# Nyström attention and top-1 experts on one core: attention instructions in a written-out order, and q and k turned by the matrix engine

## The chip, the core and the metric

The kernel runs on one core of a Trainium2 chip. A core has five engines that run their own instruction streams in order and meet at semaphores: PE (TensorE, matrix products; its weight loads are listed apart as PEld), DVE (VectorE), ACT (ScalarE), POOL (GpSimd) and SP (SyncE, which only issues transfers here). PE's products go to PSUM, a small memory of its own that DVE and ACT read; the other data lie in SBUF. Transfers run on 16 DMA engines, issued from SP's queue and from POOL's.

The metric is the device time of one execution in microseconds (us). Before the change three runs gave 570.1, 567.15 and 567.03; the median is 567.15.

## The reference

```python
# q, k, v: (8 batches, 8 heads, 576, 64) f32;  m = 32 landmarks of g = 18 rows each
q_lm = q.reshape(B, H, m, S // m, D).mean(axis=3)
k_lm = k.reshape(B, H, m, S // m, D).mean(axis=3)
A  = softmax(scale * q    @ k_lm.T)      # 576 x 32
Bm = softmax(scale * q_lm @ k_lm.T)      # 32 x 32
C  = softmax(scale * q_lm @ k.T)         # 32 x 576
Z = Bm.T / (norm1(Bm) * norminf(Bm) + 1e-6)
for _ in range(6):
    Z = 2 * Z - Z @ Bm @ Z
x = (A @ Z @ C @ v)                      # then (8 * 576 tokens, 512)
...
e_idx = argmax(x @ w_gate, axis=1)       # 8 experts, each token goes to one
h = relu(x[mask] @ w1[e]); ye = h @ w2[e]
out[mask] = gate_w[mask, None] * sigmoid(x @ w_output_gate)[mask, e, None] * ye
```

## The kernel before

**Two stages.** The attention stage makes the rows of x and writes them to a DRAM table, `x_rows`; for each batch it also finds the tokens' experts. After the last batch a short routing part (L400 to L449) sorts the tokens by expert into 43 tiles of 128 slots. The expert stage gathers one tile after another from `x_rows` (L464, POOL's queue), multiplies it by `w1` and `w2` of the tile's expert (L483, L502, bf16) and scatters the result (L509).

**The unit of the attention stage** is a half-batch: four heads of one batch, so that 4 x 32 landmarks fill 128 partitions. There are 16 units. For each unit q and k are loaded as (head and landmark) x (18 x 64) into three shared slots `nats` (L178), and `turned` makes three things of each:

- `tr`, the 32x32 blocks turned by DVE (L180). It puts 32 of the 64 columns d on the partitions of a head, in two pieces c;
- the sums over the 18 rows of a landmark, five additions on POOL (L181 to L186), turned by DVE to `lmT` (L188);
- `bd`, the same four landmark blocks spread over a 128x128 block-diagonal matrix, two products with a mask on POOL (L191).

`scores` (L205) then multiplies `bd` (128x128) with `tr` (128x288) for two halves n and two pieces c. It is called for C (landmarks of q against k) and for A (landmarks of k against q). An f32 product stands in the trace as two MATMUL records, here called passes, each with its own weight load.

**The rest of a unit.** C: maximum on DVE (L247), exponential on ACT (L250), six turns on PE (L257) and copies on ACT (L258), then the product with v, 24 small products of 96x32 by 96x64 (L262). A: turn on DVE (L270), maximum (L272), subtraction on POOL (L276), exponential on ACT (L277), sum (L278), product on POOL (L280), turn back to `AT` (L282).

**Per batch**: `Bm` (L225 to L243), seven dependent Newton steps of two products (L295) and one DVE operation (L303) on both halves at once, `ZB` (L311, POOL), the gate's logits (L317 to L338), the choice of the expert and the token's place (L344 to L369), and five products `pX` with `ZB` (L393), each copied by ACT (L396) and sent to `x_rows` (L397, SP).

**Memory used twice.** `wall` holds the weights of all eight experts. Its last parts are free until they are loaded: q, k and the sums lie in expert 7's part, v in expert 6's. `load_expert` (L73 to L82, POOL's queue, two transfers of 1 MB written and 2 MB read) is called for experts 0 to 5 after batches 0 to 5, and for 6 and 7 after the last batch's `AT`. The expert stage picks its weights by an address from a register, so its first product waits for all eight loads.

**What sets the order.** A scheduling layer orders the instructions of each engine by the program's order and its own estimate of when operands and buffers are free; nothing in the program fixes it. PSUM buffers: one for the scores of C, one for those of A, one for the turns of C (`et`), two small ones (`m`), one for `pX`.

Of the kernel before, what the change touches and what calls it, by code (L numbers as in the profile page):

```python
# [22 lines left out]
F32 = mybir.dt.float32  # L23
BF16 = mybir.dt.bfloat16
EXP = mybir.ActivationFunctionType.Exp
SIG = mybir.ActivationFunctionType.Sigmoid
RELU = mybir.ActivationFunctionType.Relu
# [9 lines left out]
def kernel(  # L37
# [98 lines left out]
    s_bm = scale / (g * g)  # L136
    s_a = scale / g
    s_c = scale / g
    KC = g // 2
    NC = KC * m  # L140
    VJ = 6
    VA = g // VJ

    with tc.tile_pool(name="attn_c", bufs=1) as cp, \
# [17 lines left out]
        for G in Gs:  # L162
# [4 lines left out]
        nats = [wall[:, E - 1, i * 2 * GD:(i + 1) * 2 * GD].bitcast(F32).rearrange("p (k d) -> p k d", d=D)  # L167
                for i in range(3)]
        t9 = wall[:, E - 1, 6 * GD:7 * GD].bitcast(F32).rearrange("p (k d) -> p k d", d=D)
        VD = HH * VJ * D  # L170
        vSs = [wall[:VA * m, E - 2, i * 2 * VD:(i + 1) * 2 * VD].bitcast(F32).rearrange(
            "p (h j d) -> p h j d", h=HH, j=VJ) for i in range(2)]
        turns = iter(range(4 * B))

        def turned(src, b, hf):

            nat = nats[next(turns) % 3]
            nc.sync.dma_start(out=nat, in_=src[b, hf * HH:(hf + 1) * HH].rearrange("h (r k) d -> (h r) k d", k=g))  # L178
            tr = sb.tile([128, g, 2, m], F32, tag="tr", bufs=3)
            nc.vector.transpose(out=tr.rearrange("p k c r -> p (k c r)"), in_=nat.rearrange("p k d -> p (k d)"))  # L180
            nc.gpsimd.tensor_tensor(t9, nat[:, 0:9], nat[:, 9:18], op=ADD)  # L181
            nc.gpsimd.tensor_tensor(t9[:, 0:4], t9[:, 0:4], t9[:, 4:8], op=ADD)
            nc.gpsimd.tensor_tensor(t9[:, 0:2], t9[:, 0:2], t9[:, 2:4], op=ADD)
            nc.gpsimd.tensor_tensor(t9[:, 0], t9[:, 0], t9[:, 1], op=ADD)
            lm = sb.tile([128, D], F32, tag="lm")
            nc.gpsimd.tensor_tensor(lm, t9[:, 0], t9[:, 8], op=ADD)  # L186
            lmT = sb.tile([128, 2, m], F32, tag="lmT", bufs=4)
            nc.vector.transpose(out=lmT.rearrange("p c r -> p (c r)"), in_=lm)  # L188
            bd = sb.tile([128, 2, HH, m], F32, tag="bd", bufs=4)
            for c in range(2):  # L190
                nc.gpsimd.tensor_tensor(  # L191
                    bd[:, c], mask,
                    lmT[:, c, :].rearrange("p (h r) -> p h r", h=1).to_broadcast([128, HH, m]), op=MUL)
            return tr, lmT, bd

        def scores(bd, tr, tag, by_j=False):

            p = ps.tile([128, 2, 512], F32, tag=tag)
            for n in range(2):
                for c in range(2):  # L200
                    if by_j:
                        rhs = tr.rearrange("p (a j) c r -> p j a c r", j=VJ)[:, n * VJ // 2:(n + 1) * VJ // 2, :, c, :]
                    else:
                        rhs = tr[:, n * KC:(n + 1) * KC, c, :]
                    nc.tensor.matmul(p[:, n, :NC], lhsT=bd[:, c].rearrange("p h r -> p (h r)"),  # L205
                                     rhs=rhs, start=(c == 0), stop=(c == 1))
            return p[:, :, :NC]

        for b in range(B):
            XW = sb.tile([128, 2, 128 + D], F32, tag="X", bufs=3)  # L210
            cc = sb.tile([128, 2], F32, tag="cc")
            ATs = []
            for hf in range(2):
                vS = vSs[hf]
                for a in range(VA):
                    nc.sync.dma_start(
                        out=vS[a * m:(a + 1) * m],
                        in_=v[b, hf * HH:(hf + 1) * HH].rearrange("h (r k) d -> r h k d", k=g)[:, :, a * VJ:(a + 1) * VJ, :])
                qT, qlmT, qBD = turned(q, b, hf)
                kT, klmT, kBD = turned(k, b, hf)  # L220


                pB = ps.tile([128, 192], F32, tag="m", bufs=2)
                for c in range(2):
                    nc.tensor.matmul(pB[:, :m], lhsT=qBD[:, c].rearrange("p h r -> p (h r)"),  # L225
                                     rhs=klmT[:, c, :], start=(c == 0), stop=(c == 1))
                st = sb.tile([128, 8], F32, tag="st", bufs=4)
                nc.vector.tensor_reduce(st[:, 0:1], pB[:, :m], axis=X, op=MAX)
                nc.vector.tensor_scalar(out=st[:, 1:2], in0=st[:, 0:1], scalar1=-s_bm, scalar2=None, op0=MUL)
                Bm = sb.tile([128, m], F32, tag="Bm")  # L230
                nc.scalar.activation(out=Bm, in_=pB[:, :m], func=EXP, scale=s_bm, bias=st[:, 1:2],
                                     accum_out=st[:, 2:3])
                nc.vector.reciprocal(st[:, 3:4], st[:, 2:3])
                nc.vector.tensor_scalar(out=Bm, in0=Bm, scalar1=st[:, 3:4], scalar2=None, op0=MUL)
                nc.gpsimd.tensor_tensor(
                    XW[:, hf, :128].rearrange("p (h r) -> p h r", r=m), mask,
                    Bm.rearrange("p (h r) -> p h r", h=1).to_broadcast([128, HH, m]), op=MUL)
                pS = ps.tile([128, 192], F32, tag="m", bufs=2)
                nc.tensor.matmul(pS[:, :m], lhsT=bones, rhs=Bm)
                nc.vector.tensor_reduce(cc[:, hf:hf + 1], pS[:, :m], axis=X, op=MAX)  # L240
                nc.vector.tensor_scalar(out=cc[:, hf:hf + 1], in0=cc[:, hf:hf + 1], scalar1=1e-6,
                                        scalar2=None, op0=ADD)
                nc.vector.reciprocal(cc[:, hf:hf + 1], cc[:, hf:hf + 1])  # L243


                pC = scores(qBD, kT, "sc", by_j=True)
                nc.vector.tensor_reduce(st[:, 4:5], pC, axis=mybir.AxisListType.XY, op=MAX)  # L247
                nc.vector.tensor_scalar(out=st[:, 5:6], in0=st[:, 4:5], scalar1=-s_c, scalar2=None, op0=MUL)
                EC = sb.tile([128, VJ, VA * m], F32, tag="EC", bufs=1)
                nc.scalar.activation(out=EC.rearrange("p (n j) q -> p n (j q)", n=2), in_=pC, func=EXP,  # L250
                                     scale=s_c, bias=st[:, 5:6], accum_out=st[:, 6:7])
                nc.vector.reciprocal(st[:, 7:8], st[:, 6:7])
                ECT = sb.tile([VA * m, VJ, 128], F32, tag="ECT", bufs=1)
                for j3 in range(2):
                    pE = ps.tile([VA * m, VJ // 2, 128], F32, tag="et")
                    for j in range(VJ // 2):
                        nc.tensor.transpose(pE[:, j, :], in_=EC[:, j3 * (VJ // 2) + j, :], identity=I128)  # L257
                    nc.scalar.copy(ECT[:, j3 * (VJ // 2):(j3 + 1) * (VJ // 2), :], pE)  # L258
                pV = ps.tile([128, 192], F32, tag="m", bufs=2)
                for j in range(VJ):  # L260
                    for h in range(HH):
                        nc.tensor.matmul(pV[h * m:(h + 1) * m, :D], lhsT=ECT[:, j, h * m:(h + 1) * m],  # L262
                                         rhs=vS[:, h, j, :], start=(j == 0), stop=(j == VJ - 1))
                nc.vector.tensor_scalar(out=XW[:, hf, 128:], in0=pV[:, :D], scalar1=st[:, 7:8],
                                        scalar2=None, op0=MUL)


                pA = scores(kBD, qT, "sa")
                At = sb.tile([128, g, m], F32, tag="At")
                nc.vector.transpose(out=At.rearrange("p (n k) r -> p n (k r)", n=2), in_=pA)  # L270
                ax = sb.tile([128, 2, g], F32, tag="ax")
                nc.vector.tensor_reduce(ax[:, 0], At, axis=X, op=MAX)  # L272

                def b_l(ap):
                    return ap.rearrange("p (k r) -> p k r", r=1).to_broadcast([128, g, m])
                nc.gpsimd.tensor_tensor(At, At, b_l(ax[:, 0]), op=SUB)  # L276
                nc.scalar.activation(out=At, in_=At, func=EXP, scale=s_a)  # L277
                nc.vector.tensor_reduce(ax[:, 1], At, axis=X, op=ADD)  # L278
# [5 lines left out]
            if b < E - 2:  # L284
                load_expert(b, ATs[1])
            elif b == B - 1:
                load_expert(E - 2, ATs[1])
                load_expert(E - 1, ATs[1])
# [264 lines left out]
```

## Time and profile before

| | us |
|---|---|
| median of three runs | 567.15 |
| the profiled execution | 568.91 |
| its span, first to last instruction | 567.2 |
| first q loaded, first work on it | 15.14 |
| first score product (L205) | 20.4 |
| `ZB` of batch 0 and of batch 7 (L311) | 64.2 and 347.0 |
| first gather of the expert stage (L464) | 368.6 |
| first product of the expert stage (L483) | 374.0 |

Busy time over the span: PE 438.5 us (77%), DVE 285.8 (50%), ACT 122.0 (22%), POOL 305.1 (54%). The granted clock of TensorE is 0.872 on average.

A line of the windows view gives a stretch, its length, then each engine's busy time with the number of instructions, the granted clock, the share of the DMA engines and GB/s. A line of the timeline gives start, duration, engine, source line, operation, output<-input, shape, and how many records were merged (x4); in brackets stands the idle time before it and what ended it. A line of the groups gives the busy time and the mean ns of one, then the idle time before and its releasers.

### The profile page before, as it was taken

The numbers are of one execution on the slowest core, as the hardware profiler recorded it, in microseconds if no ns is written. First come the engines' busy times: TensorE is split into PE (matmuls) and PEld (weight loads), VectorE is DVE, ScalarE is ACT, GpSimd is POOL, SyncE is SP. The second block draws the span as 40 slices with busy tenths as digits, with TensorE's granted clock in tenths as the row PEclk, the third lists the DMA queues.
The fourth block names the chain that finished last, engine by engine and source line by source line (L and its number), as shares of the span: only waits on it lengthen the run. The fifth ranks groups of instructions, "written<-read, shape, count | busy, mean of one in ns | idle before, by whom it ended". The sixth has DMA issues, their size and how long they took to land. (4 is left out here: it accounts for less than half of the span.)

```text
span 567.2 us, 9257 instructions
## 1 busy us (share of the span) xinstructions
PE 438.5 (77%) x3127; PEld 277.0 (49%) x3127; DVE 285.8 (50%) x748; ACT 122.0 (22%) x279; POOL 305.1 (54%) x492
## 2 busy tenths in 40 slices
PE   0458758758776867779797878559999999999992
PEld 0235545536555545448474554325555555555551
DVE  1355557657666756736764322713444444353441
ACT  0012222123131222122231211112223222232220
POOL 2667895796687678585624111353444545454422
PEclk9978969969897958877897565769999999999998
DMA  6643946935989369388044754121232323223200
GB/s 163 168 125 84 210 119 180 213 107 118 254 195 206 100 167 218 103 156 184 9 111 68 126 92 72 33 75 57 75 112 85 107 81 104 86 92 94 85 29 0
DMA packets 41726, 66.13 MB, mean 117 GB/s; under 512 B 10353, under 2 KB 29810, under 8 KB 41682
## 3 DMA queue, kind: packets, MB, share of 16 engines
q0 software_dynamic: 18048, 31.90, 26.3%
q1 hardware_dynamic: 23634, 33.64, 21.5%
q8 instruction: 27, 0.44, 0.4%
q14 instruction: 17, 0.14, 0.1%
HBM read 67.58 MB, written 16.56 MB: 148 GB/s over the span
## 5 line engine op out<-in xcount | busy, mean ns | idle before, releaser
L205 PE MATMUL p<-tr,bd 128*128 128x288 f32 x256 | 88.6, 474 | 28.5 <-DVE tr L180 21.1
L509 POOL DMA_INDIRECT out_dram<-ysb x43 | 43.5, 1012 | 93.7 <-DVE ysb L508 90.0
L483 PE MATMUL ph<-wall,xT 128*128 x344 | 82.9, 385 | 3.0 <-DVE xT L471 2.9
L502 PE MATMUL py<-wall,hT 128*128 x344 | 81.1, 379 | 0.0
L393 PE MATMUL pX<-ZB,AT 128*128 128x256 f32 (+1 forms) x160 | 63.4, 520 | 19.8 <-ACT xo L396 15.2
L487 ACT ACTIVATE h<-ph 128x512 bf16<-128x512 f32 x86 | 46.7, 594 | 144.7 <-PE ph L483 141.6
L205 PEld LDWEIGHTS p<-tr,bd 128*128 128x128 f32 x256 | 52.9, 222 | 41.4 <-POOL bd L191 29.7
L295 PE MATMUL pN<-nxt 128*128 128x192 f32 x192 | 47.8, 375 | 19.9 <-DVE nxt L303 16.8
L483 PEld LDWEIGHTS <-xT 128*128 128x128 bf16 x344 | 33.9, 99 | 45.3 <-issue 5.7
L393 PEld LDWEIGHTS pX<-ZB,AT 128*128 128x128 f32 (+1 forms) x160 | 32.7, 233 | 44.1 <-ACT xo L396 23.1
L181 POOL TENSOR_TENSOR wall<-wall 128x576 f32<-128x576 f32 x32 | 44.9, 1402 | 13.7 <-DMA wall<-in_q_dram 11.3
L295 PEld LDWEIGHTS pN<-nxt 128*128 128x128 f32 x192 | 34.8, 209 | 33.7 <-DVE nxt L303 26.6
L464 POOL DMA_INDIRECT xs<-x_rows,gat_i x43 | 41.9, 974 | 15.9 <-issue 13.4
L180 DVE STREAM_TRANSPOSE tr<-wall 128x1152 f32<-128x1152 f32 x32 | 43.3, 1352 | 12.4 <-DMA wall<-in_q_dram 11.5
L502 PEld LDWEIGHTS <-hT 128*128 128x128 bf16 x344 | 31.9, 98 | 30.7
L495 DVE COPY hT<-pht 128x1024 bf16<-128x1024 bf16 x43 | 29.7, 690 | 29.4 <-PE pht L493 23.2
L507 DVE CAST ysb<-xs 128x1 int32<-128x1 f32 x43 | 6.6, 154 | 74.7 <-issue 64.6
L191 POOL TENSOR_TENSOR bd<-mask,lmT 128x128 f32<-128x128 f32 x64 | 28.0, 456 | 25.2 <-PE p L205 11.8
L508 DVE TENSOR_SCALAR ysb<-py,xs 128x512 f32<-128x512 f32 x43 | 31.9, 743 | 4.2 <-PE py L502 3.8
L396 ACT CAST xo<-pX 128x512 bf16<-128x512 f32 (+1 forms) x40 | 23.3, 581 | 49.9 <-PE pX L393 34.4
L303 DVE SCALAR_TENSOR_TENSOR nxt<-nxt,pN 128x384 f32<-128x384 f32 x40 | 21.5, 538 | 17.9 <-PE pN L295 17.7
L276 POOL TENSOR_TENSOR At<-At,ax 128x576 f32<-128x576 f32 x16 | 18.4, 1157 | 21.1 <-DVE ax L272 21.1
(136 smaller groups left out, 607.3 us busy)
## 6 DMA issues: line engine op xcount, KB each, us to landing
wall<-in_moe_w_dram POOLq DMA_DIRECT2D x16, 1024.0 KB
wall<-in_v_dram SPq DMA_DIRECT2D x48, 192.0 KB, 4.2
wall<-in_q_dram SPq DMA_DIRECT2D x16, 576.0 KB, 5.1
wall<-in_k_dram SPq DMA_DIRECT2D x16, 576.0 KB, 5.2
x_rows<-xo SPq DMA_DIRECT2D x32, 128.0 KB, 2.8
xs<-x_rows,gat_i POOLq DMA_INDIRECT x43
out_dram<-ysb POOLq DMA_INDIRECT x43
x_rows<-St SPq DMA_DIRECT2D x1, 516.0 KB, 4.6
```

Of the source, the lines that this page charges most:

```text
L180: nc.vector.transpose(out=tr.rearrange("p k c r -> p (k c r)"), in_=nat.rearrange("p k d -> p (k d)"))
L181: nc.gpsimd.tensor_tensor(t9, nat[:, 0:9], nat[:, 9:18], op=ADD)
L205: nc.tensor.matmul(p[:, n, :NC], lhsT=bd[:, c].rearrange("p h r -> p (h r)"), rhs=rhs, start=(c == 0), stop=(c == 1))
L295: nc.tensor.matmul(pN[:, hf, :], lhsT=cur[:, hf, :128], rhs=cur[:, hf, :])
L393: nc.tensor.matmul(pX[:tk, hf * HH * D:(hf + 1) * HH * D], lhsT=ATs[hf][:, j * 128:j * 128 + tk], rhs=ZB[:, hf].rearrange("p h d -> p (h d)"))
L464: nc.gpsimd.indirect_dma_start(out=xs, out_offset=None, in_=x_rows, in_offset=bass.IndirectOffsetOnAxis(ap=gat_i[:, j:j + 1], axis=0))
L483: nc.tensor.matmul(ph[hf], lhsT=xT[:, dc, :], rhs=wf[:, bass.ds(we[j] + (dc * F + hf * 512), 512)], start=(dc == 0), stop=(dc == DCH - 1))
L487: nc.scalar.activation(out=hs[j][:, hf * 512:(hf + 1) * 512], in_=ph[hf], func=RELU)
L495: nc.vector.tensor_copy(hTs[j], pht)
L502: nc.tensor.matmul(py, lhsT=hT[:, fc, :], rhs=wf[:, bass.ds(we[j] + (W1 + fc * HD), HD)], start=(fc == 0), stop=(fc == FCH - 1))
L508: nc.vector.tensor_scalar(out=ysb[:, :HD], in0=py, scalar1=xs[:, HD // 2:HD // 2 + 1], scalar2=None, op0=MUL)
L509: nc.gpsimd.indirect_dma_start(out=out, out_offset=bass.IndirectOffsetOnAxis(ap=token, axis=0), in_=ysb[:, :HD], in_offset=None, bounds_ch ...
```

## The change

The arithmetic stays; where and when it is done changes.

- The instructions of the attention stage are cut into pieces (`turn3`, `c_scores`, `a_max`, `p_mm` and so on). Each piece gets a place on a time axis with a period P = 12.0 for a unit, and the pieces are issued in the order of their places under `manual_schedule()`, so that every engine's order is the program's. Unit u's q and k are turned during unit u-1's scores, the Newton steps of a batch run in the next two units, the logits and `pX` two units later.
- q and k are turned by PE: nine 128x128 turns each (`turn3`), three to a PSUM buffer, copied by ACT (`keep3`). A turned pair of rows has 64 columns d on 64 partitions, twice.
- The sums of k stay on POOL, those of q go to DVE (`sums`); both landmark sets are turned by PE (`turn_lm`) and scaled by ACT (`keep_lm`). `bd` and its products are gone.
- `scores` is eight products with 64 contracted rows and 32 output columns each, 288 long: two row halves by four heads, in 64x32 tiles of the array.
- Six slots for q and k instead of three (experts 7's and 5's parts); `AT` lies in expert 4's part. Experts 0 to 3 are loaded after units 1, 3, 5 and 7, experts 5, 6, 7 after the last unit, expert 4 after the last `pX`.
- PSUM buffers: two for turns (`t`), one for all scores (`s`), two small ones (`m`), one for the Newton steps (`n`), one for `pX`. Some small DVE operations are done for both halves at once; the scaling of v's product moves from DVE to ACT.

```diff
-        def turned(src, b, hf):
-            nat = nats[next(turns) % 3]
...
+        nats = [home(E - 1 - i // 3 * 2, i % 3, GD).rearrange("p (k d) -> p k d", d=D) for i in range(6)]
+        t9s = [home(e, 6, GD // 2).rearrange("p (k d) -> p k d", d=D) for e in (E - 1, E - 3)]
...
+        def sums(u, i):
+            eng, t9, nat = (nc.gpsimd, nc.vector)[i], t9s[i], nats[(2 * u + i) % 6]
+            eng.tensor_tensor(t9, nat[:, 0:9], nat[:, 9:18], op=ADD)
+            eng.tensor_tensor(t9[:, 0:4], t9[:, 0:4], t9[:, 4:8], op=ADD)
+            eng.tensor_tensor(t9[:, 0:2], t9[:, 0:2], t9[:, 2:4], op=ADD)
+            eng.tensor_tensor(t9[:, 0], t9[:, 0], t9[:, 1], op=ADD)
+            lm[u, i] = sb.tile([128, 2, D], F32, tag=f"lm{i}", name="lm")
+            eng.tensor_tensor(lm[u, i], t9[:, 0:1].to_broadcast([128, 2, D]), t9[:, 8:9].to_broadcast([128, 2, D]), op=ADD)
+        def turn3(u, i, n):
+            nat = nats[(2 * u + i) % 6]
+            if n == 0:
+                tr[u, i] = sb.tile([128, K2, 128], F32, tag="tr", bufs=4, name="tr")
+            tr[u, i, n] = pT = ps.tile([128, 3, 128], F32, tag="t", bufs=2, name="pT")
+            for k2 in range(3):
+                nc.tensor.transpose(pT[:, k2], identity=I128,
+                                    in_=nat[:, 6 * n + 2 * k2:6 * n + 2 * k2 + 2].rearrange("p k d -> p (k d)"))
+        def keep3(u, i, n):
+            nc.scalar.copy(tr[u, i][:, 3 * n:3 * n + 3], tr.pop((u, i, n)))
...
+        def scores(lms, tr, by_j=False):
+            p = ps.tile([128, 2, 512], F32, tag="s")
+            for h in range(HH):
+                for i in range(2):
+                    rhs = tr[i * D:(i + 1) * D, :, hm(h)]
+                    if by_j:
+                        rhs = rhs.rearrange("p (a c) r -> p c a r", a=VA)
+                    nc.tensor.matmul(p[hm(h), i, :NC], lhsT=lms[i * D:(i + 1) * D, hm(h)], rhs=rhs)
+            return p[:, :, :NC]
...
+        P = 12.0
+        for u in range(NU):
+            t = u * P
+            at(t - 4 * P + 11.9 if u > 2 else -30 + u, load_qk, u)
+            at(t - 2 * P + 11.9 if u > 1 else -30 + u + 0.5, load_v, u)
+            for n in range(3):
+                at(t - P + 1.5 + 0.4 * n, turn3, u, 0, n)
+                at(t - P + 2.6 + 0.5 * n, keep3, u, 0, n)
+                at(t - P + 4.9 + 0.4 * n, turn3, u, 1, n)
+                at(t - P + 5.5 + 0.5 * n, keep3, u, 1, n)
+            at(t - P + 0.1, sums, u, 0)
+            at(t - P + 1.9, sums, u, 1)
+            at(t - P + 8.5, turn_lm, u)
+            at(t - P + 8.9, keep_lm, u)
+            at(t + 0.0, c_scores, u)
+            at(t + 0.8, c_max, u)
+            at(t + 1.6, c_exp, u)
+            at(t + 3.5, a_scores, u)
+            at(t + 4.3, a_max, u)
+            at(t + 5.9, a_sub, u)
+            at(t + 7.1, a_exp, u)
+            at(t + 7.9, a_sum, u)
+            at(t + 9.0, a_mul, u)
+            at(t + P + 0.2, a_back, u)
+            for i in range(2):
+                at(t + 6.1 + 0.4 * i, c_turn, u, i)
+                at(t + 7.8 + 0.5 * i, c_keep, u, i)
+            at(t + 8.8, values, u)
+            at(t + 9.8, keep_values, u)
...
+        for b in range(B):
+            t = (2 * b + 1) * P
...
+            t += P
+            for it, place in enumerate((0.7, 4.2, 7.8, 10.5, 12.7, 16.2, 19.8)):
+                at(t + place, p_mm, b, it)
+                at(t + place + 0.9, p_next, b, it)
...
+            at(t + 2.8, logits, b)
+            at(t + 6.2, choose, b)
...
+            for j, place in enumerate((6.9, 9.8, P + 2.8, P + 6.9, P + 9.7)):
+                at(t + place, x_mm, b, j)
+                at(t + place + 1.0, x_out, b, j)
+        for e in range(E):
+            u = 2 * e + 1 if e < E - 4 else NU - 1
+            at((NU + 4) * P if e == E - 4 else u * P + P + 3.3, lambda e=e, u=u: load_expert(e, ATs[u]))
+        with tc.manual_schedule():
+            for _, _, fn, args in sorted(plan, key=lambda p: p[:2]):
+                fn(*args)
```

## The prediction

> **What bounds the kernel now.** The chain of waits ends in the last transfers and covers 0.7% of the span, so it says nothing of the attention stage. I read the windows first, cutting the span where the two stages meet.
>
> ```profile
> 15.00:374.00 359.00, 257.67 (x1927) 180.55 (x1928) 205.11 (x561) 74.03 (x192) 220.86 (x392) 0.81 0.60 136
> 374.00:567.00 193.00, 180.79 (x1200) 96.50 (x1199) 78.39 (x169) 46.67 (x86) 81.26 (x82) 0.98 0.24 78
> 333.00:346.00 13.00, 9.25 (x23) 6.71 (x24) 3.50 (x7) 0.00 (x0) 0.57 (x1) 0.50 0.99 161
> ```
>
> The columns are PE, PEld, DVE, ACT, POOL, clock, DMA share, GB/s. The expert stage (193 us) is bound by PE and the change doesn't touch it. In the attention stage no engine is full: POOL is busy 62%, PE 72% with unfinished pipelines counted, at a clock of 0.81. Next the pace, from the instructions of one line:
>
> ```profile
> L311 POOL TENSOR_TENSOR ZB<-mask,nxt x16: 712/726/731, 64.2 to 347.7; 128x256 f32<-128x256 f32 x16
> ```
>
> Batch 0's first ZB starts at 64.2, batch 7's at 347.0: 7 batches, 40.4 us each, **20.2 us per unit** (half-batch). Divided by 16 units the busy times are POOL 13.8, DVE 12.8, ACT 4.6. So waits between engines bound the stage: the fullest engine, POOL, works 68% of a period. PE's true load I take from starts in the timeline where it waits for nothing and the clock is full:
>
> ```profile
> 263.50 1.13 PE L205 MATMUL p<-tr,bd 128*128 128x288 f32 x4
> 264.48 0.49 PE L257 MATMUL pE<-I,EC 128*96 128x128 f32 x3
> 264.80 0.65 PE L205 MATMUL p<-tr,bd 128*128 128x288 f32 x2
> 265.29 0.81 PE L295 MATMUL pN<-nxt 128*128 128x192 f32 x4
> 265.94 0.49 PE L257 MATMUL pE<-I,EC 128*96 128x128 f32 x3
> ...
> 287.39 1.03 PE L393 MATMUL pX<-ZB,AT 128*128 128x256 f32 x4
> 288.26 0.65 PE L205 MATMUL p<-tr,bd 128*128 128x288 f32 x2
> ```
>
> From start to start: a score pass 0.98/4 = 0.245, a turn 0.32/3 = 0.107, a Newton pass 0.65/4 = 0.163, a pX pass 0.87/4 = 0.217. The tail of a group lies under the next one.
>
> **PE's load per unit, before and after.** Before: 16 score passes 3.9; 6 turns 0.64; 14 Newton passes 2.28; 10 pX passes 2.17; v's product 1.04 (two fences down); logits, gates, ranks and the like (half of L332's 1.28, of L324's 0.27 and of five small groups of 0.1 to 0.25) 1.15; pB 0.45. Sum 11.6. After, the score passes and pB's four go. Added are 18 turns of q and k, 2 of the landmarks, and two score calls. The trace shows no 128-column turn: 0.107 (the 96-column row) below, 0.107 x 128/96 = 0.143 above; I take 0.128, so 18 are 2.3 and 2 are 0.25. No 64x32 tile with 288 columns is there either; the nearest rows are small products side by side:
>
> ```profile
> 261.23 1.10 PE L262 MATMUL pV<-wall,ECT 96*32 96x64 f32 x48
> 262.27 0.59 PE L295 MATMUL pN<-XW 128*128 128x192 f32 x2
> ...
> 348.97 0.34 PE L324 MATMUL pG<-wgs,ZT 64*32 64x16 f32 x16
> 349.24 1.22 PE L393 MATMUL pX<-ZB,AT 128*128 128x256 f32 x2
> ```
>
> 48 passes of 64 columns take 1.04 us, 0.022 each, where one alone would need 0.245 x 64/288 = 0.054; and 16 of the 64x32 form are through in 0.27, at half clock. So tiles overlap. A call has 16 passes on 8 tiles: two rounds of 0.245 if all eight overlap, plus 0.2 for getting in and out (below the 0.27), 0.69; if none did, 3.9. I take 0.69, since the 64x32 row is the same form; two calls 1.4. After: 2.3 + 0.25 + 1.4 + 0.64 + 2.28 + 2.17 + 1.04 + 1.15 = **11.2**. PE's work hardly falls; the gain must come from waits.
>
> **The other engines per unit, after.** Rows used:
>
> ```profile
> L181 POOL TENSOR_TENSOR wall<-wall 128x576 f32<-128x576 f32 x32 | 44.9, 1402 | 13.7 <-DMA wall<-in_q_dram 11.3 <-DMA wall<-in_k_dram 0.8
> L180 DVE STREAM_TRANSPOSE tr<-wall 128x1152 f32<-128x1152 f32 x32 | 43.3, 1352 | 12.4 <-DMA wall<-in_q_dram 11.5 <-PE p L205 0.8
> L258 ACT COPY ECT<-pE 96x384 f32<-96x384 f32 x32 | 15.1, 473 | 31.1 <-PE pE L257 30.6 <-PE prk L357 0.4 <-PE pV L262 0.2
> ```
>
> *DVE* loses two turns (2 x 1.35) and two of lmT (0.48), gains q's sums: by the 0.74 of a 576-long operation (L272), 0.54 of 384 (L303) and 0.28 of 128 (L306), the five cost 0.74 + 0.40 + 0.27 + 0.20 + 0.27 = 1.9. With what stays (C's maximum 0.75, A's turns and reductions 3.3, Newton 1.75, routing and Bm 2.7) 10.5. *POOL* loses q's sums (1.40 + 0.73 + 0.46 + 0.33 + 0.32 = 3.2) and four bd products (1.8): 13.8 - 5.0 = 8.8. *ACT* gains six copies of 0.47, lmT's 0.4 and v's scaling 0.25: 8.1. *DMA*: q, k and v unchanged; six slots start them two units ahead.
>
> **The period.** In the written order all four engines fit in 12. I laid PE's order of an even unit on these prices and found where it must wait. Turns have two buffers, so the third group of k's turns waits for the first ACT copy, which stands behind C's exponential: 0.95. The third group of q's waits likewise: 0.4. C's turns wait for the same buffers: 0.2. v's product waits for the second ECT copy, which stands behind A's exponential and an xo copy: 0.45. Sum 2.0. Behind PE's wait stand pX and the Newton pass, so DVE is late with it.
>
> One wait is new: DVE's five q additions run beside POOL's five for k.
>
> ```profile
> 353.12 0.20 DVE L349 TENSOR_TENSOR oh<-row,sm 128x40 bf16<-128x40 f32 x1
> ...
> 284.04 0.82 DVE L349 TENSOR_TENSOR oh<-row,sm 128x40 bf16<-128x40 f32 x1
> ...
> 283.58 1.21 POOL L280 TENSOR_TENSOR At<-At,ax 128x576 f32<-128x576 f32 x1
> ```
>
> The same DVE instruction takes 0.20 with POOL idle and 0.82 beside a POOL operation that ends at 284.79. Bounds: 0 if they miss each other, half of POOL's 3.3 = 1.65 if each addition meets one. Behind them stands A's maximum, and POOL, ACT and PE behind that; the order leaves some slack there, I take 0.3. The Trainium skill, "SBUF — State Buffer", Who interferes with whom, says that a DVE tensor_tensor with both inputs in SBUF takes a port shared with GpSimd and the later one blocks fully; the row agrees, and by it alone I would book all 1.65, 21 us more over 16 units.
>
> *Clock.* In slices of 10 us the clock is 0.52 where PE is busy 5.5 (200 to 210) and 0.91 at 9.8 (260 to 270); in the expert stage 1.00. PE's true duty was 11.6/20.2 = 0.57 at a mean clock of 0.86 from 60 to 300; at 11.2/14.3 = 0.78, on the line to 1.00 at full duty, the clock is 0.93: 11.2/0.93 = 12.0. Bounds: 11.2 (clock 1) and 13.8 (0.81, the whole stage's). The Trainium skill, "TensorE: Matmul & The Clock Gate", Part 4: PE-mode transpose, speaks against the change: turns don't count as a busy array in the same way. By it the duty without turns is (11.2 - 3.2)/14.3 = 0.56, the clock stays 0.86, and a unit needs 13.0: 16 us more in the end. No run here shows f32 turns in such a share; bf16 turns are 12 of 28 PE instructions of the expert stage, at 1.00.
>
> Period 12.0 + 2.0 + 0.3 = **14.3**; bounds 12.0 (every wait hidden) and 13.8 + 2.0 + 1.65 = 17.4.
>
> **Before and after the periods.** k is now first on SP's queue, at 4.8 instead of v's pieces; with 5.2 to landing it is there at 10, q at 11.5; turns, copies and lmT take 4.5, so the first scores come at 16 (before 20.4). Units 0 and 1 have no Newton or pX yet: -6.
>
> At the end two paths race. *Compute*: seven Newton steps at
>
> ```profile
> 335.75 1.65 PE L295 MATMUL pN<-nxt 128*128 128x192 f32 x4 [0.65 <-DVE nxt L303]
> 338.11 1.65 PE L295 MATMUL pN<-nxt 128*128 128x192 f32 x4 [0.70 <-DVE nxt L303]
> ```
>
> 2.3 each at half clock = 16, +0.7 to begin, +5 for batch 6's pX in between; from the last step to the first gather 368.63 - 346.67 = 22, to PE 3.1: 47. *Weights*: four experts now wait for the last unit, where before there were two. The windows' third line is one expert's load alone: 13 us at a share of 0.99. The first expert product waits for all of them: 2.5 + 4 x 13 + 2 to land = **56.5** after the last period. This load was under the Newton steps before; now it is the bound, and compute has 9.5 of slack. Then 193.2 of expert stage (374.0 to the end).
>
> **Sum** against the profiled execution: 1.7 around the span + 16 - 6 + 16 x 14.3 + 56.5 + 193.2 = 490.2, where it has 568.91. The median is 1.8 lower: **488**.
>
> **Rivals.**
> - *The timetable holds at its 12 us.* For: DVE, POOL and ACT fit. Against: PE's 2 us of waits. 1.7 + 10 + 192 + 56.5 + 193.2 - 1.8 = 452. Chance 0.15.
> - *A fixed order waits as the scheduler's did.* PE at 68% of 12.0/0.68 = 17.6: 541. For: one late instruction stops its whole engine. Chance 0.12.
> - *The clock stays at half in the stage; slower.* PE then needs 22.4 + 2.0 = 24.4 a unit: 650. For: 320 to 350, clock 0.50 with PE busy 75%, waits of 0.7 between products. Against: PE would then be full, and full slices have 1.00. It decides from a period of 19.2, a mean clock of 0.66. Chance 0.08.
> - *The 64x32 tiles don't overlap.* 2 x 3.2 more a unit, 20.7: 590. Against: the L324 rows. Chance 0.04.
>
> The forecast, periods of 13 to 16.5, has 0.58; 0.03 is left for what I don't see. 0.5% is about what a measurement of this kernel tells from no change. Faster 0.86, the same 0.02, slower 0.12. Range: 452 (period 12.0) to 538 (period 17.4).
>
> **What would show it.** ZB 28 to 29 us apart per batch; score groups of 16 records within 0.7 to 0.9; DVE's q additions at 1.9 or stretched towards 3.5; PE idle before the third turn group, put down to ACT's copy; clock near 0.93; the first expert product released by a transfer into `wall`, with PE idle some 10 us. Wrong if PE's clock falls with the turns, or if periods differ from unit to unit by more than 3 us.

## The result, and the profile after

The changed kernel takes 469.9 us (468.1 to 473.1, 4 runs) where the kernel before took 568.6 in the same job: a ratio of 0.826, 95% interval 0.820 to 0.833. A second job gave 472.0 us and 0.829 (0.825 to 0.833); that second job is the yardstick for the variants below. The forecast was 488 us with a range of 452 to 538.

The profiled execution took 473.05 us. Its page begins with the busy time of each engine, its share of the span and the instructions; of the slices (a fortieth of the span each, busy share in tenths) these are PE's, DVE's, POOL's and the granted clock's:

```profile
span 471.3 us, 10353 instructions
...
PE 388.6 (82%) x3729; PEld 242.5 (51%) x3751; DVE 264.2 (56%) x676; ACT 166.2 (35%) x383; POOL 233.6 (50%) x348
...
PE   0878888888888898898685438999999999999991
...
DVE  1266787878879787987445403443444434444441
...
POOL 2566667483857547373811551444445545554231
PEclk9987999999999999999986559999999999999996
```

PE now has eights and nines from the fourth slice to the nineteenth, and from the fifth on the clock stands at nine beside them; before, no engine was full in that stage. The dip in slices 20 to 24 is the tail between the attention and the expert stage. The same in windows (PE, PEld, DVE, ACT, POOL, clock, DMA share, GB/s):

```profile
19.00:230.00 211.00, 179.02 (x2387) 125.33 (x2372) 161.48 (x415) 107.92 (x272) 127.90 (x207) 0.98 0.70 179
230.00:284.00 54.00, 29.15 (x161) 18.61 (x161) 20.30 (x72) 8.14 (x19) 21.74 (x41) 0.68 1.07 197
284.00:471.00 187.00, 174.70 (x1164) 94.67 (x1184) 77.86 (x166) 45.59 (x84) 77.72 (x78) 0.98 0.24 76
261.00:282.00 21.00, 6.75 (x51) 4.37 (x52) 4.47 (x13) 0.58 (x1) 12.11 (x13) 0.50 1.01 197
```

The stage of 16 units takes 211 us, where before they took some 323 (16 x 20.2). The last line lies in the tail: the transfers fill it at 197 GB/s while no engine is full (POOL, the busiest, works 12.1 of the 21 us). The pace, from one line's instructions (duration least/median/most in ns, first and last start):

```profile
L368 POOL TENSOR_TENSOR ZB<-mask,ZV x16: 723/730/736, 65.4 to 244.6; 128x256 f32<-128x256 f32 x16
```

Batch by batch ZB starts at 65.4, 92.7, 119.9, 147.2, 174.2, 201.3, 226.3 and 244.0: some 27.1 us apart until the work runs out, **13.56 us a unit** from unit 5 to unit 15 by C's exponentials (81.9 to 217.5). One odd unit on PE (start, us, instructions, idle before and what ended it):

```profile
190.17 0.87 PE L210 MATMUL pT<-I,wall 128*128 128x128 f32 x6
191.90 0.55 PE L210 MATMUL pT<-I,wall 128*128 128x128 f32 x3 [0.86 <-ACT tr L214]
192.28 1.03 PE L482 MATMUL pX<-ZB,wall 128*128 128x256 f32 x4
193.24 0.72 PE L234 MATMUL p<-tr,lmT 64*32 64x288 f32 x16
...
195.70 0.55 PE L210 MATMUL pT<-I,wall 128*128 128x128 f32 x3 [0.24 <-ACT tr L214]
...
199.41 0.41 PE L219 MATMUL pM<-I,lm 128*128 128x128 f32 x2 [0.55 <-ACT ECT L258]
199.75 1.20 PE L266 MATMUL pV<-wall,ECT 96*32 96x64 f32 x48
```

The waits stand where the prediction put them: ahead of the third group of k's turns, of q's third group, and ahead of what follows ACT's ECT copies (here the landmark turns, with v's product behind them). A score call of 16 records takes 0.72.

### The profile page after: what moved, and what is told of

Its sections match the earlier page's. It is cut to its first block, busy times and chain, and to the rows that moved or that the text cites. A ratio compares the mean times of both kernels' runs of the same rounds, so it can differ in the third digit from the quotient of the medians.

```text
span 471.3 us, 10353 instructions
## 1 busy us (share of the span) xinstructions
PE 388.6 (82%) x3729; PEld 242.5 (51%) x3751; DVE 264.2 (56%) x676; ACT 166.2 (35%) x383; POOL 233.6 (50%) x348
## 5 line engine op out<-in xcount | busy, mean ns | idle before, releaser
L671 PE MATMUL py<-wall,hT 128*128 x323 | 76.7, 379 | 1.1
L210 PE MATMUL pT<-I,wall 128*128 128x128 f32 x288 | 49.4, 305 | 26.5 <-ACT tr L214 13.1
L214 ACT COPY tr<-pT 128x384 f32<-128x384 f32 x96 | 43.2, 480 | 44.8 <-PE pT L210 44.7
L210 PEld LDWEIGHTS pT<-I,wall 128*128 128x128 f32 x288 | 35.9, 154 | 38.1 <-ACT tr L214 23.9
L633 POOL DMA_INDIRECT xs<-x_rows,gat_i x43 | 41.9, 974 | 15.9 <-issue 11.6
L482 PE MATMUL pX<-ZB,wall 128*128 128x256 f32 (+1 forms) x160 | 46.4, 416 | 3.9 <-ACT xo L488 3.9
L350 PE MATMUL pN<-nxt 128*128 128x192 f32 x192 | 42.4, 344 | 0.9 <-DVE nxt L359 0.8
L350 PEld LDWEIGHTS pN<-nxt 128*128 128x128 f32 x192 | 32.0, 192 | 14.1 <-DVE nxt L359 6.2
L482 PEld LDWEIGHTS pX<-ZB,wall 128*128 128x128 f32 (+1 forms) x160 | 27.4, 191 | 13.2 <-ACT xo L488 5.4
L197 POOL TENSOR_TENSOR wall<-wall 128x576 f32<-128x576 f32 x16 | 22.5, 1405 | 12.9 <-DMA wall<-in_k_dram 12.9
L662 PEld LDWEIGHTS <-h 128*128 128x128 bf16 x344 | 22.9, 98 | 11.3 <-ACT h L656 0.5
## 6 DMA issues: line engine op xcount, KB each, us to landing
wall<-in_moe_w_dram POOLq DMA_DIRECT2D x16, 1024.0 KB, 10.8
wall<-in_v_dram SPq DMA_DIRECT2D x48, 192.0 KB, 4.3
```

The lines of the kernel that those rows point to most:

```text
L210: nc.tensor.transpose(pT[:, k2], identity=I128, in_=nat[:, 6 * n + 2 * k2:6 * n + 2 * k2 + 2].rearrange("p k d -> p (k d)"))
L214: nc.scalar.copy(tr[u, i][:, 3 * n:3 * n + 3], tr.pop((u, i, n)))
L350: nc.tensor.matmul(pN[:, hf, :], lhsT=cur[:, hf, :W], rhs=cur[:, hf, :])
L482: nc.tensor.matmul(pX[:tk(j), hf * HH * D:(hf + 1) * HH * D], lhsT=ATs[2 * b + hf][:, j * 128:j * 128 + tk(j)], rhs=ZBs[b][:, hf].rearrang ...
L633: nc.gpsimd.indirect_dma_start(out=xs, out_offset=None, in_=x_rows, in_offset=bass.IndirectOffsetOnAxis(ap=gat_i[:, j:j + 1], axis=0))
L671: nc.tensor.matmul(py, lhsT=hT[:, fc, :], rhs=wf[:, bass.ds(we[j] + (W1 + fc * HD), HD)], start=(fc == 0), stop=(fc == FCH - 1))
```

## The experiments

Three questions were left. Is it the order or the new data path that makes the gain? Do PE's waits set the unit, as the sum had it? And do the weights bound the tail? Each variant is told by its edit of the changed kernel.

### Order against data path

**The new path with a free order.** The pieces are named in the plan's sequence, but the scheduler may move them:

```diff
-        with tc.manual_schedule():
-            for _, _, fn, args in sorted(plan, key=lambda p: p[:2]):
-                fn(*args)
+        for _, _, fn, args in sorted(plan, key=lambda p: p[:2]):
+            fn(*args)
```

> The changed kernel with its new data path (TensorE turns, 64x32 tiles, k's sums on POOL and q's on DVE) but without the fixed order: the scheduler may order the instructions again, as it did before the change. Theory (the fixed order is most of the gain): the busiest engine has some 11.7 us a unit in the changed kernel; before, a unit took 20.2 us with 13.8 us on its busiest engine, 1.46 times as much. At that factor a unit takes 17.1 us in place of 13.5, so 473 + 16 x 3.6 = 530 us, range 505 to 560. Rival (the new data path alone makes the gain, by taking work from DVE and POOL): units stay within 1 us of 13.5, so 470 to 490 us.

Measured: 475.2 us, ratio 0.835 (0.831 to 0.839), units of 14.1. The theory fell. Taking the fixed order away cost about 3 to 5 us, and its interval overlaps that of the changed kernel in both jobs.

**The changed kernel again**, as the yardstick:

> The changed kernel once more, as the yardstick for the small differences among the variants. The kernel with free order took 0.8352 of the kernel before, the changed one 0.8263. If the fixed order is worth anything here, this run stays at 0.82 to 0.83; if the two are equal within what can be measured, it comes to 0.833 to 0.838.

Measured: 472.0 us, 0.829 (0.825 to 0.833). Fixing the order is worth about 1% here by the medians, and the intervals don't tell it from nothing.

**The old path in the fixed order.** In place of the turns, `turn` is a DVE transpose, both sums stand on POOL, the landmarks are turned by DVE and spread over a block diagonal by POOL, and `scores` is again full-array:

```diff
-                at(t - P + 1.5 + 0.4 * n, turn3, u, 0, n)
...
+            at(t - P + 1.5, turn, u, 0)
+            at(t - P + 2.5, sums, u, 1)
+            at(t - P + 5.5, turn_lm, u, 0)
+            at(t - P + 6.0, turn, u, 1)
+            at(t - P + 7.0, keep_lm, u, 0)
+            at(t - P + 8.4, turn_lm, u, 1)
+            at(t - P + 9.1, keep_lm, u, 1)
```

> The fixed order, three units deep, with the old data path: q and k turned by DVE, both sums and the block-diagonal landmarks on POOL, scores as full-array products. Theory (order is most of the gain): POOL is full again with some 13.8 us a unit, and a fixed order leaves 0.3 to 1.5 us of waits, so units of 14.1 to 15.5 us: 473 + 16 x (0.6 to 2.0) = 483 to 505 us. Rival (the data path makes the gain): units of 18 us and more, 545 us and above.

Measured: 532.2 us, 0.934 (0.929 to 0.938), units of 17.0 (a tenth of the time between the second and the seventh batch's ZB). It lies between the two, so neither theory holds alone. The places are mine, fitted to the new path's other pieces and not tuned for this one.

**The old path with a free order**, the same pieces in the same sequence:

> The old data path with the plan's sequence and a free scheduler; the fixed order of the same pieces took 532 us with POOL's and DVE's landmark work late for the scores. Theory (the scheduler orders as well as the plan does once the pieces are named in the plan's sequence): 515 to 545 us. Rival (without the fixed order the old path falls back to the kernel before): 555 to 575 us.

Measured: 517.3 us, 0.910 (0.905 to 0.914), units of 15.0, within the theory's range. Here the scheduler does better than my fixed order, by 15 us.

**The new path in the sequence of the kernel before.** All buffers stay as they are in the changed kernel; the pieces are named batch by batch, half by half, and the scheduler is free:

```diff
+        for b in range(B):
+            for u in (2 * b, 2 * b + 1):
+                load_v(u)
+                load_qk(u)
...
+                c_scores(u)
...
+                a_back(u)
...
+            for it in range(7):
+                p_mm(b, it)
+                p_next(b, it)
...
```

> The new data path alone: the program names the pieces batch by batch in the order of the kernel before, and the scheduler is free. Theory (the data path makes the gain, since the kernel with the plan's sequence but a free scheduler took only 475 us): 470 to 495 us. Rival (the sequence in which the program names the pieces, three units deep, makes the gain, and the free scheduler followed it): units of 16 us and more as before, 510 to 550 us.

Measured: 551.2 us, 0.967 (0.962 to 0.972), units of 18.7; the time is 1 us over the rival's range. So the theory that the data path alone makes the gain falls too, and the rival holds. Together:

| us (ratio to before) | old data path | new data path |
|---|---|---|
| sequence of before, scheduler free | 569.5 (the kernel before) | 551.2 (0.967) |
| plan's sequence, scheduler free | 517.3 (0.910) | 475.2 (0.835) |
| plan's sequence, order fixed | 532.2 (0.934) | 472.0 (0.829) |

The data path alone is worth 18 us, the sequence alone 52, both 94. The sequence is worth 76 once the new path is there, and the path 42 once the sequence is there. The first cell isn't pure: the five variants also hold the change's small merged steps (one Bm per batch, v's scaling on ACT) and its deeper buffers; before doesn't. So the 18 and the 52 us hold what these add, while the 76 and the 42 stand between variants that share them. Deeper buffers by themselves don't make the gain: the kernel with them and the new path, in the old sequence, still takes 18.7 us a unit (20.2 before). Whether the plan's sequence needs them wasn't run. How the waits look in the old sequence, on DVE:

```profile
228.43 1.91 DVE L197 TENSOR_TENSOR wall<-wall 128x576 f32<-128x576 f32 x1
230.38 0.83 DVE L198 TENSOR_TENSOR wall<-wall 128x256 f32<-128x256 f32 x1
231.24 0.43 DVE L199 TENSOR_TENSOR wall<-wall 128x128 f32<-128x128 f32 x1
231.70 0.30 DVE L200 TENSOR_TENSOR wall<-wall 128x64 f32<-128x64 f32 x1
231.92 0.74 DVE L243 TENSOR_REDUCE st<-p 128x1 f32<-128x576 f32 x1
```

and on PE of the same kernel:

```profile
228.76 0.72 PE L234 MATMUL p<-tr,lmT 64*32 64x288 f32 x16
233.59 1.52 PE L253 MATMUL pE<-I,EC 128*96 128x128 f32 x6 [4.11 <-ACT EC L247]
```

C's scores are done by 229.5, but their maximum starts on DVE only at 231.92, behind sums that a later unit needs, and PE stands idle for 4.11 us. The scheduler keeps near to the sequence in which the pieces are named. In the plan's sequence three units' pieces alternate, so that each has other units' work between its links.

### Does PE set the unit?

**Every score call twice.** The eight products are issued a second time with the same result:

```diff
                     nc.tensor.matmul(p[hm(h), i, :NC], lhsT=lms[i * D:(i + 1) * D, hm(h)], rhs=rhs)
+            for h in range(HH):
+                for i in range(2):
...
+                    nc.tensor.matmul(p[hm(h), i, :NC], lhsT=lms[i * D:(i + 1) * D, hm(h)], rhs=rhs)
```

> The eight products of each score call are issued twice, with the same result; it prices a call in 64x32 tiles and shows whether TensorE sets the period. By the trace a call of 16 passes takes 0.51 to 0.65 us on TensorE, so two more calls are 1.0 to 1.3 us a unit. Theory (TensorE with its waits bounds the unit): the whole of it shows, 473 + 16 x 1.15 = 491 us, 487 to 496. Rival (the chain through DVE bounds, at least in the odd units): half of it or less, 473 to 482. If the four tiles ran one after another, a call would cost some four times as much and the time would be over 530.

Measured: 476.9 us, 0.836 (0.833 to 0.840), 5 us over the yardstick; units of 14.1, so 0.5 more each. In windows of the doubled kernel and then of the changed one:

```profile
90.00:217.00 127.00, 114.06 (x1712) 81.31 (x1705) 97.14 (x259) 66.34 (x169) 75.45 (x129) 1.00 0.64 163
```

```profile
90.00:217.00 127.00, 109.99 (x1497) 78.15 (x1499) 101.88 (x267) 68.62 (x175) 75.99 (x129) 1.00 0.65 167
```

Divided by 127/14.08 and 127/13.56 units, PE's busy time is 12.65 and 11.74: two calls cost PE 0.91, so 0.46 each, and about 0.5 of the 0.9 reaches the unit. The rival's "half of it" fits the better. PE's waits give some way, so they were not all on the chain.

**The third group of k's turns later**, behind the A scores, so that PE need not wait for its buffer:

```diff
-                at(t - P + 1.5 + 0.4 * n, turn3, u, 0, n)
-                at(t - P + 2.6 + 0.5 * n, keep3, u, 0, n)
+                at(t - P + (1.5, 1.9, 3.7)[n], turn3, u, 0, n)
+                at(t - P + (2.6, 3.1, 4.3)[n], keep3, u, 0, n)
```

> k's third group of turns stands behind the A scores instead of ahead of them, and its copy 0.7 later on ACT, so that TensorE need not wait there for ACT's first copy (0.86 us in the odd units, about as much in the even ones by the trace). Theory (that wait is on the chain that sets the period, as the prediction counted it with 0.95): the unit falls by 0.5 to 0.9, so 8 to 14 us: 457 to 464, a ratio of 0.805 to 0.815. Rival (TensorE's waits take up slack that another chain leaves, since only half of a doubled score call showed): 466 to 472, 0.82 to 0.83.

Measured: 471.7 us, 0.826 (0.822 to 0.830). Nothing, as the rival had it: the units are 13.56 from unit 5 to 14, as before the edit. PE's waits from 90 to 198 us (us in total, times, longest), first in the yardstick, then here:

```profile
PE pT L210 <- ACT tr L214: 8.0, 16, 0.9
PE pV L266 <- ACT ECT L258: 2.8, 4, 0.8
PE pM L219 <- ACT ECT L258: 2.2, 4, 0.6
PE pE L253 <- ACT tr L214: 0.8, 4, 0.2
```

```profile
PE pM L219 <- ACT ECT L258: 5.3, 8, 1.0
PE pV L266 <- ACT ECT L258: 4.7, 4, 1.2
PE pT L210 <- ACT tr L214: 1.9, 8, 0.2
```

The waits for `tr` fell by 6.1, and those for `ECT` rose from 5.0 to 10.0. PE came earlier to the next stop and waited there.

**C's copies first on ACT.** That stop is made on ACT. In the changed kernel, in the unit shown above:

```profile
196.29 0.48 ACT L214 COPY tr<-pT 128x384 f32<-128x384 f32 x1 [0.25 <-PE pT L210]
198.22 0.68 ACT L293 ACTIVATE At<-At 128x576 f32<-128x576 f32 x1 [1.46 <-POOL At L290]
198.81 0.46 ACT L258 COPY ECT<-pE 96x384 f32<-96x384 f32 x1
199.17 0.58 ACT L488 CAST xo<-pX 128x512 bf16<-128x512 f32 x1
199.65 0.48 ACT L258 COPY ECT<-pE 96x384 f32<-96x384 f32 x1
```

ACT stands 1.46 us ahead of A's exponential, which waits for POOL, while C's turns, issued from 196.26, are done by about 197.4 and their copies queue behind it. The edit:

```diff
-                at(t + 7.8 + 0.5 * i, c_keep, u, i)
+                at(t + 7.0 + 0.05 * i, c_keep, u, i)
```

> On ACT the two copies of the turned C half stand ahead of the exponential of the A half, which waits for POOL's subtraction until 198.2 in the unit looked at while the turns behind it were done by 197.2. Theory (v's product and with it the unit's end hang on these copies, some 1 us later than need be in the odd units): the odd unit falls by up to 1 us, 8 us in all: 462 to 468, a ratio of 0.812 to 0.823. Rival (DVE's chain through the A half sets the odd unit, and gets its exponential later): 470 to 476, 0.825 to 0.837.

Measured: 462.7 us, 0.811 (0.807 to 0.815), units of 12.7. The gain is a little above the theory's 8 us, and the even units fell as well (12.8 from 13.7). ACT in that kernel:

```profile
187.40 0.48 ACT L214 COPY tr<-pT 128x384 f32<-128x384 f32 x1 [0.25 <-PE pT L210]
187.95 1.02 ACT L258 COPY ECT<-pE 96x384 f32<-96x384 f32 x2
189.47 0.68 ACT L293 ACTIVATE At<-At 128x576 f32<-128x576 f32 x1 [0.49 <-POOL At L290]
```

The copies fill the idle time, and A's exponential still starts 0.49 after ACT is free. PE's waits for `ECT` are gone from the list; the third group's are the same 7.9.

**q's sums on POOL**, where k's are:

```diff
-            eng, t9, nat = (nc.gpsimd, nc.vector)[i], t9s[i], nats[(2 * u + i) % 6]
+            eng, t9, nat = (nc.gpsimd, nc.gpsimd)[i], t9s[i], nats[(2 * u + i) % 6]
...
-            at(t - P + 1.9, sums, u, 1)
+            at(t - P + 3.2, sums, u, 1)
```

> q's five additions go from DVE to POOL, where k's are, some 1.3 us later in the order. DVE loses 2.35 us a unit, POOL gains about 3.6 (k's own additions take 1405 + 751 + 618 + 380 + 485 ns there), so POOL has some 12.5 to 13 us a unit. Theory (TensorE with its waits bounds the unit, DVE does not): no gain, 470 to 478 us, or more where q's landmarks come late for their turn. Rival 1 (DVE bounds the odd units): they get shorter by 0.5 us and more, 460 to 468. Rival 2 (POOL becomes the bound with its waits, 14 to 14.5 us a unit): 481 to 490.

Measured: 484.5 us, 0.850 (0.846 to 0.853). The units alternate: 12.5 for the odd ones and 14.4 for the even ones in the second half, up to 18.6 for an even one before. Both rivals hold, each for its units: taking 2.35 us from DVE shortens the odd unit by 0.9, and in the even one POOL is nearly full (busy 12.4 of the 14.4 us from 187.8 to 202.2).

**q's sums on POOL for the even units alone**, which run during the odd ones:

```diff
+            eng, t9, nat = (nc.gpsimd, nc.vector)[i * u % 2], t9s[i], nats[(2 * u + i) % 6]
...
+            at(t - P + (3.2, 1.9)[u % 2], sums, u, 1)
```

> q's additions go to POOL for the even units alone; they run during the odd units, which took 12.5 us in place of 13.4 with all of them on POOL, while the even ones took 14.4. Theory (DVE with its queue sets the odd units, TensorE with its waits the even ones): odd units 12.5, even ones 13.6, a batch 26.1 in place of 26.9 to 27.0: 8 x 0.9 = 7 us less, 463 to 466, a ratio of 0.815 to 0.82. Rival (the odd units were short there only because the even ones ran long and left work done ahead): 469 to 473, 0.825 to 0.833.

Measured: 474.2 us, 0.831 (0.827 to 0.835), by the time the rival (1 us over its range, the ratio within it). But the units are as the theory has them, 12.5 and 13.6, and ZB starts every 26.0 us. What they gained was lost at the start: from the third unit's C exponential to the fourth's there are 17.3 us. There, on POOL (the first expert's load, and A's subtraction behind it):

```profile
46.30 0.84 POOL L79 CAST wall<-wall 1x1 bf16<-1x1 f32 x2
52.20 1.00 POOL L80 DMA_DIRECT2D wall<-in_moe_w_dram  x1 [5.06 <-issue]
53.20 0.95 POOL L82 DMA_DIRECT2D wall<-in_moe_w_dram  x1
54.14 1.19 POOL L290 TENSOR_TENSOR At<-At,ax 128x576 f32<-128x576 f32 x1
```

POOL stood 5.06 us ahead of the load's issue, and A's chain behind it. For what it waited, the trace doesn't show.

### Do the weights bound the tail?

**The last weights early.** The last two units' ATs move to a free `tr` buffer, so that expert 4's home is free one batch earlier, and experts 5 and 7 are loaded once the last q and k have been read:

```diff
-            ATs[u] = home(E - 4, u % 7, S)
+            if u == NU - 2:
+                last2 = sb.tile([128, 2, S], F32, tag="tr", bufs=4, name="last2")
+                ATs[NU - 2], ATs[NU - 1] = last2[:, 0], last2[:, 1]
+            elif u < NU - 2:
+                ATs[u] = home(E - 4, u % 7, S)
...
+            place = {E - 3: 15 * P + 4, E - 1: 15 * P + 9.2, E - 2: 16 * P + 3.3, E - 4: 17 * P + 10.8}
+            at(place.get(e, u * P + P + 3.3), lambda e=e, u=u: load_expert(e, ATs[u]))
```

> The last four experts' weights are loaded as soon as their homes are free: experts 5 and 7 during the last two units, expert 6 behind them, and expert 4 some 20 us earlier, since the last two A halves lie in a buffer of their own. Theory (the tail is bound by four loads of about 13 us each, then the gathers): the loads end by some 255 us in place of 279, the first gather lands right behind its issue at 270, the first expert product starts at 272 to 274 in place of 279.3: 463 to 466 us. Rival (the computing path, with the routing done at 268.7, bounds the tail just as much): 468 to 470. Rival 2 (two loads of 1 MB during the units delay k, q and v, or the rows written out): the units get longer, 470 and above.

Measured: 467.6 us, 0.822 (0.819 to 0.825), 4.3 under the yardstick, between the ranges of the theory and of the rival. PE at the start of the expert stage, first in the yardstick, then here:

```profile
276.05 0.58 PE L638 MATMUL pt<-Ib,xs 128*128 128x128 bf16 x4 [11.07 <-DMA xs<-x_rows,gat_i]
277.83 2.72 PE L652 MATMUL ph<-wall,xT 128*128 x6 [1.19 <-DVE ysb L676]
```

```profile
271.86 0.58 PE L643 MATMUL pt<-Ib,xs 128*128 128x128 bf16 x4 [6.86 <-DMA xs<-x_rows,gat_i]
274.24 3.57 PE L657 MATMUL ph<-wall,xT 128*128 x8 [1.80 <-DVE xT L645]
```

From the first gather's issue to the first expert product it takes 5.4 us (268.8 to 274.2), and 10.8 in the yardstick (267.0 to 277.8). So the weights were the bound there, and with them out of the way the computing path is, since the gathers themselves were issued no earlier. What PE waits for by name is the gathered rows (`xs`): they came late while the loads ran.

**Together**: C's copies first, the third group later, the weights early, experts 5 and 7 now at `15 * P + 0.1` and `15 * P + 0.2`.

> C's copies first on ACT, k's third group of turns behind the A scores, and the last experts' weights early (experts 5 and 7 now in the place on POOL that the sums of a unit 16 would have). By itself the later third group moved nothing, but since C's copies come first the wait ahead of it is the only one of size that TensorE has left (7.9 us in 8.5 units). Theory (what TensorE waits for is now on the chain): units of 12.0 to 12.2 in place of 12.7, so 8 to 11 us, and 4 to 6 at the tail: 446 to 451, a ratio of 0.782 to 0.792. Rival (DVE, with some 11.3 us a unit and 11.9 in the odd ones, sets the unit now): 0 to 0.3 a unit and the tail's 4 to 6: 453 to 459, 0.794 to 0.806.

Measured: **451.4 us, 0.791 (0.788 to 0.794)**, the fastest version. The time lies at the upper end of the theory's range, but the units are 12.6 in place of 12.7, so the rival is right for them; the tail gave more than either expected, from C's last exponential to the first expert product 53.9 us in place of 62.3. PE and DVE from 90 to 198 us, and PE's largest waits:

```profile
90.00:198.00 108.00, 98.87 (x1335) 71.85 (x1336) 96.14 (x243) 62.56 (x163) 73.12 (x120) 1.00 0.75 189
```

```profile
PE pG L388 <- ACT ZT L383: 2.3, 3, 0.8
PE pT L210 <- ACT tr L214: 2.2, 9, 0.2
PE prk L430 <- POOL cum L423: 1.4, 3, 0.6
PE pS L341 <- DVE Bm L333: 1.1, 4, 0.3
```

In 108/12.62 = 8.6 units PE has 11.6 us a unit and DVE 11.2. No large wait is left, the small ones are for three other engines, and both PE and DVE are near the 12.6. In the tail, part of the gain has no single cause: the last batch's ZB starts 13.5 us after the one before, where with C's copies first alone it starts 19.1 after. Two things differ there, and no run tells them apart: of the three loads issued just ahead of the routing counts on POOL one is left there, and the clock is 1.00 (214 to 228) in place of 0.73 (216 to 235).

## Why the prediction was right, and where it was not

The time fell in the range, 17 us under the forecast by the profiled execution (473.05 against the sum of 490.2). By its terms:

- **First scores at 16:** 18.4. k landed at 11.8 and q at 15.1 in place of 10 and 11.5; SP took 2.08 us to issue the first k. +2.4.
- **Period 14.3:** 13.56, with the light first units as booked (15 periods of 13.56 less 6.4). 16 x 0.74 = -12, with the half microsecond of the light units. Of the 0.74, 0.26 is PE's work by the clock, 0.2 its waits, and 0.3 the term for q's sums: in the trace work and waits alone fill the unit (11.74 + 1.82), so that term had no place beside them.
  - *PE's work 11.2:* 11.74 by busy time in the windows, which holds some unfinished pipelines. The sum left out pB, which is still there as 16 small passes a batch (0.26 us by its starts, 189.91 to 190.17, so 0.13 a unit). The calls in 64x32 tiles, booked at 0.69, cost 0.46 by doubling; they overlap, and that rival is out.
  - *Clock 0.93:* 1.00 from 90 to 217 us. I had 12.0 us for PE's work by the clock and it took 11.74. That this missed by 0.3 only is luck, since two errors nearly cancel: 0.5 too little for the work, and for that work some 0.9 too much for the clock. The line from duty to clock was drawn through averages of the kernel before, whose work came in bursts, and the same busy share stands beside different clocks: PE is busy 0.80 of the time at a clock of 0.87 in the new path with the old sequence (100 to 250 us) and 0.80 at 0.92 in the old path with a free order (90 to 240). What does set it no run here tests. The rule against the change ("TensorE: Matmul & The Clock Gate", Part 4: PE-mode transpose, in the Trainium skill, by which turns don't count as a busy array) didn't show either: the turns of q and k, of C and of the landmarks were busy 24.8 + 9.4 + 4.0 = 38.2 of PE's 110.0 us from 90 to 217, their tails counted, which leaves (110.0 - 38.2)/127 = 0.57 of the time for the other products, no more than the duty that I had for all of PE before, and the clock stayed full. No run has turns with fewer other products, so how far this goes stays open. For the rival of a half clock I read 320 to 350 as 0.50; that window shows 0.56.
  - *PE's waits 2.0:* 108 us hold 14.5 of idle PE, 1.8 a unit, at the places named. The size was right and the meaning wrong. I added four waits as if each lengthened the unit by itself. Without the third group's, booked at 0.95, the unit stayed the same; v's product behind ACT's copies, booked at 0.45, was worth 0.83 a unit when the copies went first.
  - *Blocking of q's sums 0.3:* the five additions take 2.35 on average and 1.98 by their shortest, so 0.37. The full 1.65 of the port rule in the Trainium skill ("SBUF — State Buffer", Who interferes with whom) needs every addition to meet one of POOL's; most missed, since the medians of the five lie near their shortest (0.80 against 0.75 and 0.49 against 0.42 for the two longest, the other three within 0.002). As a load on DVE the sums did matter, since the odd unit was 0.9 shorter without them.
- **Tail 56.5, bound by the weights:** 50.3 (from the end of the 16 periods, 18.4 + 210.6 = 229.0, to 279.3). The bound was right, as the early loads show; the first three loads were issued from 228.1 on and not 2.5 behind the period, the transfers slacked off at 277, 49 us after that first issue, and compute wasn't 9.5 short of it but about 5. The sign that I gave came only in part: PE stood idle 9.77 us, but for the gathered rows and not for a transfer into `wall`.
- **Expert stage 193.2:** 192.0.

Sum of the differences: 2.4 - 12.2 - 6.2 - 1.2 = -17.2, which is 490.2 to 473.

One sign of being wrong showed once: from C's fourth exponential to the fifth it takes 11.1 us and from the fifth to the sixth 14.7 (67.1 to 81.9), where the first batch's `pX` set in; from there on neighbouring units differ by 0.5. The cause of the long one stays open.

The forecast said that PE's work would hardly fall and the gain would come from waits; that holds. It credited the written order with it; the runs put that credit on the *sequence*, in which three units' pieces alternate, together with the path: with both a free scheduler comes within about 1%, and neither alone gives more than 52 of the 94 us. The rival by which a fixed order waits as the scheduler's did is out for this path. For the old path its sign was right: there the fixed order took 15 us more than the free one.

## What to carry to other kernels

Before an order is fixed by hand, name the pieces in the sequence in which they should run, several units deep: the scheduler followed it here, and fixing the order as well was worth about 1% on the new path and cost 15 us on the old one. Idle time of the fullest engine is not a list of prices: take the wait away that stands last on the chain, here a copy queued behind an instruction that waited for another engine, and only then see whether the next one counts. Look at each in-order queue for an instruction whose input comes late while ready ones stand behind it.

## What the runs showed of the hardware

- PE's clock was 1.00 through a stage in which f32 turns were 38.2 of PE's 110.0 busy us (90 to 217 us), and 0.50 where PE was busy 6.75 of 21 us (261 to 282).
- A score call of 16 records in 64x32 tiles of 288 columns costs PE 0.46 us more when it is doubled, less than two single full-array passes of the kernel before (2 x 0.245 by its starts).
- The same DVE addition of 576 elements took 0.75 us by itself and 1.19 beside POOL:

```profile
191.11 0.75 DVE L197 TENSOR_TENSOR wall<-wall 128x576 f32<-128x576 f32 x1
...
204.27 1.19 DVE L197 TENSOR_TENSOR wall<-wall 128x576 f32<-128x576 f32 x1
```

- Gathers issued while weight loads ran landed some 7.6 us after their issue (269.8, first data at 277.4; the transfers moved 203 to 210 GB/s from 270 to 274), and some 3 us after it where the weights had been loaded earlier (268.8 and 271.9; 35 GB/s from 269 to 271).
